# Storing the second product's weight forms three steps later

## The chip, the core and the metric

The kernel runs on one core of a Trainium2 chip. The metric is the device time of one execution in microseconds (us); the time of a kernel is the median of its runs. Profiles are taken from one execution; times in them count from the first instruction.

## What is computed

Attention with normalised queries and keys, and behind it a feed-forward layer with a squared ReLU. Inputs are float32, but the two weight matrices are float64.

```python
batch, n_heads, seq, head_dim = (8, 12, 448, 64)
q_n, k_n = (rmsnorm(q, g_q), rmsnorm(k, g_k))
scores = (1 / sqrt(head_dim)) * matmul(q_n, k_n.T)
attn = softmax(scores)                       # 1e-9 added to the sum
x = matmul(attn, v)                          # -> (8 * 448, 12 * 64) = (3584, 768)
h = maximum(x @ w_in, 0.0)                   # w_in  (768, 2048)
out = h * h @ w_out                          # w_out (2048, 768)
```

## The kernel before

**Attention and feed-forward interleaved.** Attention goes over 48 pairs of heads (8 batches of 6 pairs). The feed-forward layer works on two batches at a time (a group, `u` = 0 to 3), and for each group over 4 blocks of 512 hidden units. While TensorE works at the feed-forward layer of one group, the attention of later batches is woven between its matmuls. Only the first 13 pairs run with no feed-forward work beside them (`visit_alone`, up to about 140 us).

**Weight forms.** Both products of the feed-forward layer use a scheme in which four quadrants are multiplied with seven products in place of eight. It needs sums and differences of the weight quadrants, the "forms". A tile of forms of the second product, `out_sb[t]` with t = 0 to 7, is 128 x 8 x 384 float32: 4 quadrants and 4 derived forms, 1536 KB. Two tiles go with each block. `out_sb` has two buffers.

**How a tile is made, in the first group only.** Weights come as 64-bit words. `load_weights` (L1293) loads one quadrant into one of three buffers `words` (L1300 for w_in, L1305 for w_out); `split_words` takes the words apart on ScalarE (L1319 to L1321); `join_words` and `end_join` put a float32 together on VectorE (L1332, L1352, L1356). This is `convert`, once for each of 64 quadrants. After the fourth quadrant of a tile, `make_weight_forms` puts four sums into `sums_to_make` and, for a tile of the second product, one store into `forms_to_store`. `make_sum` then issues one sum a call (L1432, in turn on VectorE and GpSimd) and, when no sum is left, one store (L1434), from `out_sb[t]` to `out_forms[t]` in DRAM. The later groups read the forms back with `load_out` (L901, 24 loads), the first of them behind the last matmul of the first group. Forms of the first product are kept likewise in `in_deep`, with `deep_steps` (L1382 and L1384 the ready forms, L1392 a derived form on VectorE, L1410 its store).

**Steps.** Everything is issued in an order that the Python code fixes; each engine takes its own instructions in that order. All transfers but a few at the start are issued by SyncE's queue (SP), in order, and one that waits for a semaphore holds those behind it. There are two kinds of step:

- `begin(step)`, four times a pair while attention is alone: two calls of `make_sum`, then `follow_loads`, then `convert` where it is due.
- one round of `run(until)`, for every feed-forward product of 6 to 30 units of cost: a product's matmuls, a step of `deep_to_make`, `make_sum`, `follow_loads`, `end_join`, `convert` where due, loads of x rows (L805), attention tasks, and a few queued transfers of q, k and v (`follow_transfers`, shown as L325; while attention is alone they are issued at once, shown as L317).

**Counters.** `follow_loads` lowers the count of every entry of `to_load` and of `later` and issues those that have come to zero, first loads of words, then `later`, always from the head. `later` otherwise holds saves of x tiles (count 4, L731), stores of finished rows (count 2, L1264) and the `load_out` calls (count 4).

```python
        for some in later:
            some[0] -= 1
        while later and later[0][0] <= 0:
            later.popleft()[1]()
```

**What stands behind the weights.** ScalarE also computes the exponentials of attention (L453), VectorE also the accumulation of the second product (L1259), and TensorE waits for both to free its banks. Matmuls are L1024 and L970 (first product), L1202 and L1140 (second), L445 and L434 (scores), L535 and L549 (times v), L584 and L601 (sums of weights).

Of the kernel before, what the change touches and what calls it, by code (L numbers as in the profile page):

```python
# [224 lines left out]
def program(ctx, tc, rows, v, g, wide, ones, moe_w_in, moe_w_out, out, shift):  # L225

    nc = tc.nc
# [1056 lines left out]
    words, targets, sums_to_make, forms_to_store = {}, {}, deque(), deque()  # L1284
# [133 lines left out]
    def make_all_deep():  # L1418
        while any(callable(some) for some in sums_to_make):
            make_sum()  # L1420
        while deep_to_make:
            deep_to_make.popleft()()
# [3 lines left out]
    def make_sum():  # L1426

        if sums_to_make and callable(sums_to_make[0]):
            sums_to_make.popleft()()
        if sums_to_make:  # L1430
            to, left, right, op = sums_to_make.popleft()
            next(sum_engines).tensor_tensor(out=to, in0=left, in1=right, op=op)  # L1432
        elif forms_to_store:
            nc.sync.dma_start(*forms_to_store.popleft())  # L1434

    pieces, begun = iter(range(len(all_pieces) + 1)), []

# [13 lines left out]
    to_load, later = deque(), deque()  # L1451
# [52 lines left out]
    def run(until):  # L1504
        nonlocal spent, slowly
        slowly = True
        while spent < until:
            cost = next(stream)
            spent += cost
            if deep_to_make:  # L1510
                deep_to_make.popleft()()
            make_sum()
            follow_loads()
            end_join()
            while first and late and late[0] <= spent:
                late.popleft()
                convert()
            arrive()
            follow_plan(2 if first else 1)
            most = 2 if cost > COST_OUT else 1  # L1520
            run_tasks(most, 2 + len(transfers) // 8)
# [27 lines left out]
    def begin(step):  # L1549
        for _ in range(2):  # L1550
            make_sum()
        follow_loads()
        while early and early[0] <= step:
            early.popleft()
            convert()
            end_join()
# [247 lines left out]
```

## Time and profile before

| | us |
|---|---|
| median of 3 runs | 1425.24 |
| lowest and highest run | 1421.85, 1431.42 |
| profiled execution | 1425.5 |
| its span, first to last instruction | 1423.4 |
| mean granted TensorE clock | 0.993 |

The stretches of the profiled execution in which the stores lie, from the stage table (busy us of an engine in each stretch; the DMA share is the mean busy share of the 16 DMA engines):

| stretch, us | TensorE busy | VectorE busy | granted clock | DMA share |
|---|---|---|---|---|
| 80 to 100 | 20.00 of 20 | 18.02 | 1.00 | 0.47 |
| 100 to 120 | 16.47 of 20 | 14.97 | 0.83 | 0.68 |
| 120 to 140 | 19.44 of 20 | 15.50 | 1.00 | 0.60 |
| 260 to 280 | 19.63 of 20 | 17.53 | 1.00 | 0.93 |
| 280 to 300 | 15.37 of 20 | 15.73 | 1.00 | 0.71 |
| 360 to 380 | 17.33 of 20 | 17.60 | 0.91 | 0.92 |
| 380 to 400 | 18.89 of 20 | 12.93 | 1.00 | 0.61 |
| 460 to 480 | 18.43 of 20 | 18.88 | 1.00 | 0.94 |
| 480 to 500 | 18.11 of 20 | 12.25 | 0.83 | 0.85 |
| 500 to 1423 | 907.20 of 923 | 468.80 | 1.00 | 0.49 |

A row of a timeline reads: start, length, engine, line, operation, out<-in, shapes, how many, and in brackets the engine's idle time before it and what ended it. SPq is SyncE's queue; its length is the time of issuing, not that of the transfer.

### The profile page before, as it was taken

The numbers are of one execution on the slowest core, as the hardware profiler recorded it, in microseconds if no ns is written. First come the engines' busy times: TensorE is split into PE (matmuls) and PEld (weight loads), VectorE is DVE, ScalarE is ACT, GpSimd is POOL, SyncE is SP. The second block draws the span as 40 slices with busy tenths as digits, with TensorE's granted clock in tenths as the row PEclk, the third lists the DMA queues.
The fourth block names the chain that finished last, engine by engine and source line by source line (L and its number), as shares of the span: only waits on it lengthen the run. The fifth ranks groups of instructions, "written<-read, shape, count | busy, mean of one in ns | idle before, by whom it ended". The sixth has DMA issues, their size and how long they took to land.

```text
span 1423.4 us, 19419 instructions
## 1 busy us (share of the span) xinstructions
PE 1377.7 (97%) x6336; PEld 850.8 (60%) x6336; DVE 841.4 (59%) x1675; ACT 587.6 (41%) x1126; POOL 784.3 (55%) x778
## 2 busy tenths in 40 slices
PE   7998999989899999999999999999999999999998
PEld 3333444434344467585776758566675858778694
DVE  4997567877877775355455665445544565254444
ACT  6775456645546234433342434444243403221230
POOL 5666755564645696465485777655673554030311
PEclk9999999999999999999999999999999999999999
DMA  5555745966768957373654747465551716234132
GB/s 147 142 152 157 202 106 143 258 171 180 205 181 244 272 149 242 73 233 90 194 153 153 222 108 229 131 190 137 151 164 27 276 57 243 108 106 174 45 145 80
DMA packets 378931, 229.15 MB, mean 161 GB/s; under 512 B 271940, under 2 KB 347588, under 8 KB 374724
## 3 DMA queue, kind: packets, MB, share of 16 engines
q1 hardware_dynamic: 378528, 227.75, 55.2%
q8 instruction: 52, 0.85, 0.2%
q14 instruction: 59, 0.48, 0.1%
q10 hardware_dynamic: 292, 0.07, 0.0%
HBM read 172.49 MB, written 55.25 MB: 160 GB/s over the span
## 4 chain that ended last, share of the span: by engine, by line
PE 63%; POOL 3%; DVE 2%; DMA 2%; issue 2%; SPq 1%; ACT 1%; DVEq 0%; POOLq 0%; ACTq 0%
PE bank L1202 25%; PE bank L1024 20%; PE bank L1140 5%; PE bank L549 4%; PE bank L434 4%; PE bank L445 2%; PE bank L970 1%; POOL sum L472 1%; PE bank L535 1%; DMA in_sb<-in_deep 1%; PE bank L610 1%; PE bank L570 1%; DMA out_sb<-out_forms 0%; DVE acc L1259 0%; SPq L325 0%
## 5 line engine op out<-in xcount | busy, mean ns | idle before, releaser
L1024 PE MATMUL bank<-xT,in_sb 128*128 128x224 f32 x1344 | 289.5, 354 | 5.1 <-DMA in_sb<-in_deep 2.8
L1202 PE MATMUL bank<-out_sb,hid 128*128 128x384 f32 x768 | 271.0, 489 | 7.5 <-DVE acc L1259 5.8
L1259 DVE TENSOR_TENSOR acc<-acc,bank 128x384 f32<-128x384 f32 x324 | 173.0, 548 | 157.4 <-PE bank L1202 137.7
L1024 PEld LDWEIGHTS bank<-xT,in_sb 128*128 128x128 f32 x1344 | 252.4, 190 | 17.6 <-ACT wT L453 5.6
L453 ACT ACTIVATE wT<-bank,rr 128x448 f32<-128x448 f32 x288 | 164.1, 631 | 137.3 <-PE bank L434 74.3
L1202 PEld LDWEIGHTS bank<-out_sb,hid 128*128 128x128 f32 x768 | 144.5, 190 | 113.1 <-DVE acc L1259 9.8
L1202 PE MATMUL bank<-out_sb,sums 128*128 128x384 f32 x576 | 206.1, 490 | 1.7 <-DVE acc L1259 1.5
L203 POOL TENSOR_TENSOR rr<-ms,minus_half 128x8 f32<-128x8 f32 (+1 forms) x96 | 149.3, 1555 | 99.9 <-DVE ms L196 98.5
L1009 DVE TENSOR_TENSOR hid<-hid,bank 128x224 f32<-128x224 f32 x312 | 111.4, 384 | 87.8 <-PE bank L1024 83.5
L1202 PEld LDWEIGHTS bank<-out_sb,sums 128*128 128x128 f32 x576 | 107.7, 190 | 86.3 <-issue 4.2
L970 PE MATMUL bank<-xT,in_sb 128*128 128x448 f32 x336 | 131.9, 546 | 0.0
L472 POOL TENSOR_TENSOR sum<-sum,wT 128x448 f32<-128x448 f32 (+1 forms) x96 | 111.7, 1182 | 18.8 <-ACT wT L453 17.0
L1077 POOL TENSOR_TENSOR hid<-hid 128x448 f32<-128x448 f32 x24 | 27.4, 1141 | 160.2 <-DVE hid L1009 156.2
L445 PE MATMUL bank<-qT,kT 64*128 64x448 f32 (+1 forms) x492 | 107.1, 585 | 8.5 <-ACT qT L368 3.8
L472 POOL TENSOR_TENSOR sum<-wT 128x448 f32<-128x448 f32 x48 | 57.7, 1225 | 103.7 <-ACT wT L453 103.7
L970 PEld LDWEIGHTS bank<-xT,in_sb 128*128 128x128 f32 x336 | 62.1, 190 | 69.0 <-issue 62.5
L1140 PE MATMUL bank<-out_sb,hid 128*128 128x384 f32 x256 | 88.8, 493 | 0.0
L1081 ACT ACTIVATE hid<-hid 128x448 f32<-128x448 f32 x96 | 55.0, 573 | 75.3 <-DVE hid L1009 51.8
L193 DVE TENSOR_REDUCE ms<-squares 128x8 f32<-128x512 f32 (+1 forms) x68 | 41.8, 615 | 64.5 <-ACT squares L180 64.5
L445 PEld LDWEIGHTS bank<-qT,kT 64*128 64x128 f32 (+1 forms) x492 | 36.7, 170 | 71.1 <-issue 40.4
L1024 PE MATMUL bank<-more,in_sb 128*128 128x224 f32 x288 | 75.2, 355 | 3.2 <-DVE hid L1009 1.8
L434 PE MATMUL bank<-qT,kT 64*64 64x448 f32 x552 | 76.1, 541 | 0.8 <-ACT wT L453 0.8
(135 smaller groups left out, 2012.0 us busy)
## 6 DMA issues: line engine op xcount, KB each, us to landing
out_sb<-out_forms SPq DMA_DIRECT2D x24, 1536.0 KB, 9.7
in_sb<-in_deep SPq DMA_DIRECT2D x64, 384.0 KB, 3.8
in_sb<-in_deep SPq DMA_DIRECT2D x80, 256.0 KB, 4.1
words<-in_moe_w_in_dram SPq DMA_DIRECT2D x32, 384.0 KB, 3.7
words<-in_moe_w_out_dram SPq DMA_DIRECT2D x32, 384.0 KB, 3.5
out_forms<-out_sb SPq DMA_DIRECT2D x8, 1536.0 KB, 6.2
qk<-in_q_dram SPq DMA_DIRECT2D x96, 96.0 KB, 2.6
qk<-in_k_dram SPq DMA_DIRECT2D x96, 96.0 KB, 2.6
```

Source lines behind the costliest of these rows:

```text
L203: self.nc.gpsimd.tensor_tensor(out=self.rr[i][:, x, 0 : self.count(i)], in0=ms, in1=self.minus_half.to_broadcast(list(ms.shape)), op=ALU.pow,)
L434: nc.tensor.matmul(sc[ds(half * D, D)], lhsT=turned[i, 1][ds(e * D, D), ds(m * P + half * D, D)], rhs=turned[i, 0][ds(e * D, D), :], start ...
L445: nc.tensor.matmul(sc[some], lhsT=turned[p, 1][r, keys], rhs=turned[p, 0][r, :], start=True, stop=True,)
L453: nc.scalar.activation(new_weights((i, m), e), sc, AF.Exp, scale=rows.rr[i][:, 1, 2 * m + e : 2 * m + e + 1],)
L472: nc.gpsimd.tensor_tensor(out=sums[i, e][some], in0=left[some], in1=weights[key_of(i, m), e][some], op=ALU.add)
L549: nc.tensor.matmul(bank[ds(e * D, D), :], lhsT=values[i][keys, n, e, :], rhs=weights[(i, n), e][keys], start=n == 0, stop=n == NJ - 1 and ...
L970: nc.tensor.matmul(ps, lhsT=w_sb[:, IN.index(left), c, :], rhs=forms[u, c][right], start=first and c == 0, stop=c == NK - 1, skip_group_ch ...
L1009: nc.vector.tensor_tensor(out=quarter(name, n), in0=quarter(base, n), in1=ps, op=ALU.add)
L1024: nc.tensor.matmul(ps, lhsT=left, rhs=right, start=start, stop=stop, skip_group_check=True)
L1140: nc.tensor.matmul(ps, lhsT=hid[a].rearrange("p t e s -> p t (e s)")[:, t, ds(NT * P, P)], rhs=w_sb[t][:, 2 * a + half, :], start=(a, t) = ...
L1202: nc.tensor.matmul(ps, lhsT=lefts[left][:, t, ts(tt, P)], rhs=w_sb[t][:, OUT.index(right), :], start=first and t == 0, stop=t == 1, skip_g ...
L1259: nc.vector.tensor_tensor(out=acc, in0=acc, in1=ps, op=ALU.add)
```

## The change

One line of `make_sum` changes. The store of a tile is no longer issued there; it is put into `later` with a count of 3, and `follow_loads` issues it.

```diff
@@ -1431,7 +1431,7 @@
             to, left, right, op = sums_to_make.popleft()
             next(sum_engines).tensor_tensor(out=to, in0=left, in1=right, op=op)
         elif forms_to_store:
-            nc.sync.dma_start(*forms_to_store.popleft())
+            later.append([3, partial(nc.sync.dma_start, *forms_to_store.popleft())])
 
     pieces, begun = iter(range(len(all_pieces) + 1)), []
 
```

All eight stores take the new way, and nothing else is edited.

## The prediction

> **What bounds the kernel now.** I read the page first (busy times, slices, DMA issues), then the waits by engine, then the timeline around each of the eight stores, and last the stage table of the stretches in which TensorE stood still.
>
> ```profile
> PE 1377.7 (97%) x6336; PEld 850.8 (60%) x6336; DVE 841.4 (59%) x1675; ACT 587.6 (41%) x1126; POOL 784.3 (55%) x778
> ...
> PE   7998999989899999999999999999999999999998
> ...
> out_forms<-out_sb SPq DMA_DIRECT2D x8, 1536.0 KB, 6.2
> ...
> words<-in_moe_w_in_dram SPq DMA_DIRECT2D x32, 384.0 KB, 3.7
> ```
>
> TensorE is busy 1377.7 of 1423.4 us, so every stall of all kinds together is 45.7 us. The stores lie between 98.5 and 486.4 us; after that none is left, so the change can only act on what TensorE loses in about a third of the span. A store moves 1536 KB and lands in 6.2 us (248 KB per us); it is four times a load of weight words (384 KB, 3.7 us).
>
> I number the stores 0 to 7 by the tile they keep. They start at 98.54, 129.11, 270.07, 293.48, 365.37, 391.56, 459.06 and 486.35 us. Only two of them hold the queue by their own wait; the waits of SP between 90 and 100 us show the long one:
>
> ```profile
> SPq L1434 <- POOL out_sb L1432: 6.3, 1, 6.3
> ```
>
> The queue reached store 0 at 92.2 us and stood until the last sum on POOL was done at 98.5. What that costs is seen in the timeline behind it:
>
> ```profile
> 107.90 0.53 SPq L1305 DMA_DIRECT2D words<-in_moe_w_out_dram  x1
> ...
> 111.29 0.55 ACT L1319 ACTIVATE words<-words 128x384 f32<-128x384 f32 x1 [7.96 <-DMA words<-in_moe_w_out_dram]
> ...
> 112.74 1.14 ACT L453 ACTIVATE part<-bank,rr 128x448 f32<-128x448 f32 x2
> ...
> 113.41 4.08 PE L445 MATMUL bank<-qT,kT 64*128 64x448 f32 x12 [3.15 <-ACT part L453]
> ```
>
> The load of words was issued late, ScalarE stood 7.96 us for it, the exponentials queued behind it on ScalarE came late, and TensorE stood 3.15 us for them. The stage table for the same place shows a second cost (columns: stretch, length, busy PE, PEld, DVE, ACT, POOL, granted clock, DMA share, GB/s):
>
> ```profile
> 112.00:114.00 2.00, 0.59 (x2) 0.56 (x3) 0.00 (x0) 1.97 (x5) 0.00 (x0) 0.78 0.90 196
> 114.00:116.00 2.00, 2.00 (x8) 0.71 (x10) 0.08 (x1) 2.00 (x5) 0.00 (x0) 0.50 0.74 200
> ...
> 118.00:120.00 2.00, 2.00 (x12) 0.34 (x12) 1.97 (x4) 1.45 (x3) 1.82 (x3) 0.51 0.00 0
> ```
>
> After the stall the granted clock is 0.5 for six microseconds.
>
> **Where each store goes.** The count of 3 is lowered in the same call in which the store is queued, so the store leaves two calls of `follow_loads` later, behind that call's load of words. Counted along the code, and set beside SP's rows: store 0 passes eleven loads of v, q and k and the words load at 107.90. Store 1 passes nothing, since no transfer is issued in the two `begin` calls it waits: its place in the queue is the same. Stores 2, 4 and 6 are queued in the first products; each passes two in_deep stores of derived forms, four transfers of the attention inputs, and one words load (2 and 4) or two loads of x rows (6); each then stands just ahead of the last three in_deep stores. Stores 3, 5 and 7 pass three or four loads of q/k, and 3 and 5 also one words load and the save of an x tile, which was queued earlier and goes first. No entry of `later` holds a store back: the saves waiting there fall due in the step in which the store is queued. ScalarE, VectorE, POOL and TensorE keep their instructions and order. The forms are read back from 528 us on, and the two buffers of out_sb are written again some 40 us after a store, so no reader moves.
>
> **Store 0: a gain.** With the store gone from its place, SP can go on at 94.4, when the matmul on the old v tile (93.44 + 0.97) frees its buffer, instead of 98.96: the words load at 107.90 comes at about 107.90 - 4.5 = 103.4. Its buffer has been free since 97.6 (VectorE's last step on the words three pieces before). Landing 3.4 us later, as it did, gives 106.8, against 111.3. ScalarE's exponentials then end near 109.4 and TensorE, free at 110.26, does not wait: 3.15 us gone. The slow clock goes with it: twelve matmuls took 4.08 us against 2.70 for the same twelve at 90.81, the next four 1.76 against 0.92, and some 0.5 more in the following sums, 2.7 us in all. Against it: store 0 now stands ahead of the next words load (108.52 before, about 104 now), which lands behind it near 104 + 6.2 = 110.2; it is wanted near 115.75 - 5.9 = 109.9. I take off 0.9. **-5.0**, bounds -5.9 and -3.0 (if the clock still drops). *On the clock:* the Trainium skill (TensorE: Matmul & The Clock Gate, Part 1) says that the clock halves after an idle window of some 3.4 us and comes back after as long a busy one. By it the slow stretch would cost about 1.7 us, which would make this term -4.0. The rows show six microseconds at 0.5 behind a stall of 3.15 us, so I keep 2.7.
>
> **Store 2: a loss.** These are the rows behind it:
>
> ```profile
> 270.07 0.45 SPq L1434 DMA_DIRECT2D out_forms<-out_sb  x1
> ...
> 277.63 0.47 SPq L1410 DMA_DIRECT2D in_deep<-more  x1
> ...
> 281.20 0.51 SPq L1300 DMA_DIRECT2D words<-in_moe_w_in_dram  x1
> ...
> 285.22 0.56 ACT L1319 ACTIVATE words<-words 128x384 f32<-128x384 f32 x1 [3.60 <-DMA words<-in_moe_w_in_dram]
> ...
> 286.73 1.15 DVE L1332 TENSOR_SCALAR in_sb<-words 128x384 uint32<-128x384 uint32 x1
> ...
> 288.39 1.92 PE L1202 MATMUL bank<-out_sb,sums 128*128 128x384 f32 x4 [1.54 <-DVE acc L1259]
> ```
>
> The store moves to just behind 277.63. From 270 to 285 us the DMA engines are full, as their slices between 262 and 290 us (0.7 us each) show, and they were not quite full just before:
>
> ```profile
> DMA  7800939999579999999899999898989990000599
> ```
>
> What was issued from 270 to 277.6 without the store is 192 (v) + 192 + 384 (words) + 32 + 112 + 192 + 112 = 1.2 MB, 4.9 us of work in 7.5. So 2.6 us of full transfer is given up, and the words load of 281.20 lands at about 287.8 instead of 285.2. ScalarE's step on them ends at 288.4; VectorE, which took it at 286.73, comes 1.7 us late to the accumulation behind it, for which TensorE already waits (1.54). **+1.7**, bounds 0 (SP was slowed by the store, 1.3 us and more for single issues at 272.39 and 274.04, and may now be earlier) and +5 (the stall grows past the 2.45 us after which the clock fell to 0.5 at 376, costing some 2.7 more).
>
> **Store 4: nothing.** The same shift of 2.6 to 3 us meets the words load of 376.41, used at 380.45 by ScalarE, but by VectorE only at 386.26: about 5 us of cover, made by VectorE's own queue. Without that cover it costs 3. Bounds 0 and +3.
>
> **Store 6: a small loss.** It now stands ahead of three in_deep stores and nine loads of the first deep weights (2.5 MB, first used at 523). Behind them the load of k at 476.09 ended a wait of VectorE of 1.81 us at 481.88; 2.6 us more delays accumulations that TensorE needs next at 489.75, which ended at 484.3. **+1.0**, bounds 0 and +4.
>
> **Stores 1, 3, 5, 7: nothing.** Words at 298.20 and 397.19 go ahead of the store and land earlier; ScalarE stood 2.13 and 2.66 us for them, but TensorE is not behind that. Bounds -1 and 0 together.
>
> Sum: -5.0 + 1.7 + 0 + 1.0 = -2.3. The profiled execution took 1425.5 us, 2.1 more than its span, and would take 1423.2; the median of the runs is 1425.24, 0.3 under it, so **1422.9 us**. Own bounds: -5.9 - 1 = -6.9 and -3 + 5 + 3 + 4 = +9, so 1418 to 1434.
>
> **Rivals.** *No effect (about 1425):* the store still fills the engines for as long, and what is won at 110 us is lost to the words load behind the moved store. For it: every transfer stays. Against it: SP's 6.3 us wait surely goes.
>
> *Slower:* the moved stores 2, 4 and 6 stand straight ahead of loads that are wanted at once, and each passes its whole 6.2 us on, through ScalarE's or VectorE's in-order queue, to TensorE, with a clock drop of 2.7 each: 3 x 8.9 - 5 = +21.7, 1447 us. For it: three of the tightest stretches (15.4 of 20 us busy at 280 to 300) lie there, and ScalarE's waits for words total 48.0 us. Against it: the store only shifts by 8 us inside a run of transfers that is full anyway, and ScalarE has 4.87 us to spare at 296.74. It decides when words land more than 4 us later than now at two of the three places.
>
> *Faster by more:* all stalls near stores are due to their transfers and go: 5.9 at store 0, 4.5 between 284 and 293, 2.5 and 1.2 of clock at 375, 1.1 at 390, 3.2 and 2.9 of clock at 480 to 488: 21.3, 1404 us. Against it: the releasers named there are VectorE's accumulation, qT and a POOL sum, not a DMA.
>
> **How the numbers follow.** Forecast 0.52, no effect 0.23, slower 0.15, faster by more 0.10. About one per cent, 14 us, is what a measurement of this kernel can tell from no change. The first two lie within it, and a hundredth of each of the others: faster 0.09, within 0.77, slower 0.14. The range takes my own bounds, widened by the spread of the three runs (-3.4 and +6.2 about their median) and towards the two outer cases: 1413 to 1437.
>
> **What would show it.** Right: SP issues words near 103.4 instead of 107.90, the stall of 3.15 us at 113 and the 0.5 clock behind it are gone, store 0 no longer waits for POOL, store 1 still does; ScalarE's wait for words at 285 grows by about 2.6 us. Wrong: a new TensorE stall of over 4 us between 280 and 300 or 375 and 390 (the slower rival), or the stall at 113 still there with another releaser (no effect).

## The result, and the profile after

| | before | after |
|---|---|---|
| median, us (21 runs each) | 1425.24 | 1421.82 |
| lowest and highest run | 1421.85, 1431.42 | 1417.31, 1425.84 |
| profiled execution, us | 1425.5 | 1423.5 |
| its span | 1423.4 | 1421.7 |
| mean granted clock in it | 0.993 | 0.994 |

The ratio of after to before is 0.9973, with a 95% interval of [0.9962, 0.9984]: 3.4 us less at the medians, with an interval that lies below 1. The forecast was 1422.9.

The page of the changed kernel, its busy times, TensorE's slices and the stores' row:

```profile
PE 1377.9 (97%) x6336; PEld 851.7 (60%) x6336; DVE 839.5 (59%) x1675; ACT 587.3 (41%) x1126; POOL 783.7 (55%) x778
...
PE   7999999999899998999999999999999999999998
...
out_forms<-out_sb SPq DMA_DIRECT2D x8, 1536.0 KB, 6.3
```

The sums say almost nothing: busy times are the same, a store lands as slowly as before. In TensorE's row four slices differ from before: the fourth (107 to 142 us) was 8 and is 9, the ninth (284 to 320) too, and the fourteenth (462 to 498) and the sixteenth (533 to 569) were 9 and are 8. A slice says where to look, not what was won there: a TensorE with a slow clock is busy as well. So the ninth rises with a slow clock, and the fourteenth falls with less of it.

The changed kernel's timeline there, rows of SP, ScalarE and TensorE (start, length, engine, line; the idle time before, and its releaser, in brackets). L1462 is the line in `follow_loads` that issues what waits in `later`, and so the stores:

```profile
94.13 1.22 SPq L317 DMA_DIRECT2D vt<-in_v_dram  x2
...
101.26 0.53 SPq L1305 DMA_DIRECT2D words<-in_moe_w_out_dram  x1
101.89 0.38 SPq L1462 DMA_DIRECT2D out_forms<-out_sb  x1
103.41 0.38 SPq L1300 DMA_DIRECT2D words<-in_moe_w_in_dram  x1
...
105.04 0.59 ACT L1319 ACTIVATE words<-words 128x384 f32<-128x384 f32 x1 [2.07 <-DVE out_sb L1332]
...
112.02 0.97 PE L445 MATMUL bank<-qT,kT 64*64 64x448 f32 x4 [0.26 <-DVE qT L408]
```

SP goes on at 94.13 with no store in its way. The load of words that stood at 107.90 is issued at 101.26. ScalarE starts on those words at 105.04 where it was 111.29, and what it waited for is no longer the transfer, but VectorE. TensorE's stall of 3.15 us has become 0.26, with another releaser.

SP's waits in the same place, of the changed kernel, now hold one line for a store, and it is store 1 at 123.22:

```profile
SPq L1462 <- POOL out_sb L1432: 1.7, 1, 1.7
```

The stage table of the changed kernel (columns as in the prediction's):

```profile
112.00:114.00 2.00, 1.98 (x12) 0.57 (x16) 1.90 (x5) 1.68 (x4) 1.25 (x1) 1.00 0.52 176
114.00:116.00 2.00, 2.00 (x20) 0.62 (x14) 1.97 (x5) 0.15 (x1) 1.82 (x3) 1.00 0.22 51
...
284.00:288.00 4.00, 2.23 (x4) 0.91 (x4) 3.86 (x6) 1.56 (x3) 3.37 (x3) 0.52 0.34 53
```

The clock stays at 1.00 at 112 to 116 us, and TensorE does 20 matmuls in the stretch in which it did 8. But at 284 to 288 us the clock is 0.52, where the kernel before had 1.00 in all of 280 to 300.

To see where time comes and goes, I took the start of the same matmul in two profiles, the kernel's and that of before (TensorE's order is the same in all kernels of this study), and the difference of the two. The columns are times in the profile of before; the numbers are us that TensorE's work is ahead (negative) or behind:

```
at, us              108    122    160    180    283    295    470    600
after             -0.35  -5.68  -5.89  -5.58  -5.59  -3.62  -3.64  -1.97
store 0 alone     -0.34  -5.67  -5.88  -5.81  -5.82  -5.83  -5.85  -5.58
all but store 0   -0.63  -1.86  -2.29  -2.13  -2.15  -0.50  -0.51  -0.66
wait kept         -0.04  -3.47  -3.25  -3.35  -3.38  -1.92  -1.91  -1.78
store 0 by POOL   -0.16  -5.48  -5.70  -5.78  -5.79  -4.15  -4.14  -4.07
second copies     -0.16  -5.48  -5.69  -5.64  -5.64  -4.27  -4.28  -3.44
words first       -0.59  -6.00  -6.21  -6.25  -6.25  -6.25  -6.23  -8.49
stores 0 and 1    -0.36  -5.69  -5.90  -5.85  -5.87  -5.88  -5.87  -5.36
count 8           -0.18  -5.50  -5.71  +0.62  +0.61  +2.62  +2.59  +1.15
store 1 late      -0.19  -5.51  -5.72  -0.40  -0.42  +1.44  +1.40  +3.94
late but store 1  -1.25  -6.58  -6.79  -6.75  -6.76  -5.11  -5.12  -2.64
```

In the changed kernel 5.3 us are won between 108 and 122 us, and 2.0 are given back between 283 and 295. Nothing happens at store 4 or before store 6 (295 to 470). Another 1.7 go until 600 us, on balance: 1.3 are won behind 480, where the clock is slow for 3.4 us in place of 6.8 behind the same stalls, and 3.0 are lost near 555. The other rows are the experiments.

### The profile page after: what moved, and what is told of

Same layout as the page of the kernel before. It is cut to its first block, busy times and chain, and to the rows that moved or that the text cites. A ratio compares the mean times of both kernels' runs of the same rounds, so it can differ in the third digit from the quotient of the medians.

```text
span 1421.7 us, 19421 instructions
## 1 busy us (share of the span) xinstructions
PE 1377.9 (97%) x6336; PEld 851.7 (60%) x6336; DVE 839.5 (59%) x1675; ACT 587.3 (41%) x1126; POOL 783.7 (55%) x778
## 4 chain that ended last, share of the span: by engine, by line
PE 62%; POOL 4%; DVE 3%; issue 2%; DMA 2%; SPq 1%; ACT 1%; DVEq 0%; POOLq 0%; ACTq 0%
PE bank L1202 25%; PE bank L1024 20%; PE bank L1140 5%; PE bank L549 4%; PE bank L434 4%; POOL sum L472 2%; PE bank L445 1%; PE bank L970 1%; SPq L325 1%; DMA in_sb<-in_deep 1%; PE bank L610 1%; PE bank L535 1%; PE bank L570 1%; POOL xT L689 1%; DMA xT<-x_rows 0%
```

## The experiments

Kernels of one group ran on the same chip beside the kernel before: its median was 1425.44 us (32 runs) for the first four, 1424.55 (26) for the next four and 1424.33 (23) for the last two. In the edits, `t` is the number of the store.

**Store 0 alone.**

```diff
-            later.append([3, partial(nc.sync.dma_start, *forms_to_store.popleft())])
+            some, t = forms_to_store.popleft(), next(tiles_stored)
+            if t == 0:
+                later.append([3, partial(nc.sync.dma_start, *some)])
+            else:
+                nc.sync.dma_start(*some)
```

> Only store 0 goes through the count of 3; stores 1 to 7 stay where they were before. Theory (the gain is store 0's, the other seven cost a little): the whole gain of 4 to 5 us stays and the loss of 1 to 2 us behind stores 2 and 6 is not paid, so 4 to 6 us below the kernel before, ratio about 0.9965. Rival (the gain is spread over the eight stores): about an eighth to a half of 3.4 us, ratio 0.9985 or more. In the trace: no 3.15 us stall at 113 us, clock 1.00 between 112 and 120 us, and the same stalls as before from 260 us on, shifted.

Measured: 1420.61 us, ratio 0.9966 [0.9954, 0.9978]. Store 0 alone gives at least as much as all eight.

**All but store 0.** The same with `if t > 0`.

> Store 0 stays where it was; stores 1 to 7 go through the count of 3. Theory: the gain is gone and what stores 2, 4 and 6 cost is left: 0 to 3 us above the kernel before, ratio 1.000 to 1.002. Slower rival of the prediction (each of the three passes its whole transfer on): 14 us or more above, ratio 1.01. Gain spread over all: 2 to 3 us below, ratio 0.998. In the trace the 3.15 us stall at 113 us is there again with the clock at 0.5 behind it.

Measured: 1425.44 us, 0.9997 [0.9983, 1.0012]. The other seven give no gain, but they do not show the loss of 2.7 us either that the prediction's terms for stores 2 and 6 add up to: the interval reaches from -2.4 to +1.7. The stall at 113 us is back, and behind it the clock is slow for a shorter time than before:

```profile
112.88 3.93 PE L445 MATMUL bank<-qT,kT 64*128 64x448 f32 x12 [3.24 <-ACT part L453]
```

```profile
112.00:114.00 2.00, 1.12 (x3) 0.81 (x4) 0.00 (x0) 2.00 (x5) 0.00 (x0) 0.78 0.75 163
114.00:116.00 2.00, 2.00 (x10) 0.30 (x8) 0.62 (x1) 2.00 (x5) 0.00 (x0) 0.50 0.74 224
116.00:118.00 2.00, 2.00 (x16) 0.36 (x12) 1.90 (x6) 1.97 (x5) 1.65 (x1) 0.87 0.00 0
```

TensorE loses 1.2 us less there than in the kernel before (-0.63 to -1.86 in the table), with a stall that is no shorter.

**The change with the wait kept.** A store of 4 KB of the same tile stands at store 0's old place. It needs the same last sum of POOL, so SP stands as before, and the large store goes three steps later.

```diff
+            if t == 0:
+                nc.sync.dma_start(mark, some[1][:, 7, 0:8])
+            later.append([3, partial(nc.sync.dma_start, *some)])
```

> All eight stores go through the count of 3, but at the old place of store 0 SyncE issues a store of 4 KB out of the last sum of the same tile, so the queue still stands there for the sum on POOL, and the 1536 KB move later all the same. Theory (it is the wait in the queue that cost): the stall at 113 us comes back, SP issues the words load near 107.5 us again, time as e2, 0 to 3 us above the kernel before. Rival (the 1536 KB ahead of the words load cost): the stall is gone as in the change, 3 to 4 us below the kernel before; half and half: words load late by 4 us but landed sooner, stall about 1.5 us.

Measured: 1422.66 us, 0.9985 [0.9971, 0.9999]: neither all nor nothing. Its timeline (its lines from L256 on are one higher, from L1425 on two or more):

```profile
98.50 0.33 SPq L1438 DMA_DIRECT2D mark<-out_sb  x1
98.93 1.22 SPq L318 DMA_DIRECT2D vt<-in_v_dram  x2
...
106.06 0.53 SPq L1306 DMA_DIRECT2D words<-in_moe_w_out_dram  x1
...
109.76 0.56 ACT L1320 ACTIVATE words<-words 128x384 f32<-128x384 f32 x1 [6.46 <-DMA words<-in_moe_w_out_dram]
...
111.91 2.96 PE L446 MATMUL bank<-qT,kT 64*128 64x448 f32 x12 [1.69 <-ACT part L454]
```

SP stands until 98.50, as in the kernel before. But the eleven loads behind it take 7.1 us to issue (98.93 to 106.06), against 8.9 (98.96 to 107.90) behind the large store. So store 0 delayed the words in two ways: by 4.5 us for POOL's sum, and by 1.8 us because the loads behind it were issued more slowly. The second is what this kernel wins. Its stage table has one more surprise:

```profile
112.00:114.00 2.00, 2.00 (x10) 0.88 (x12) 0.19 (x1) 2.00 (x5) 0.00 (x0) 1.00 0.96 312
114.00:116.00 2.00, 2.00 (x15) 0.46 (x16) 1.51 (x4) 1.42 (x3) 0.61 (x1) 1.00 1.29 288
```

Behind a stall of 1.69 us the clock is not lowered at all. So 1.8 us of earlier issue are worth 3.4 in the table of offsets (108 to 122 us): 1.5 of stall, and the slow clock.

**Store 0 issued by GpSimd at its old place**, all else as before. The transfer is not delayed; only SP does not stand for it.

```diff
+            (nc.sync if t else nc.gpsimd).dma_start(*some)
```

> Store 0 is issued at its old place in the program, but by GpSimd, whose own sum it waits for, so SyncE does not stand and yet the 1536 KB start near 98.5 us; stores 1 to 7 as before. Theory (the wait in SyncE's queue cost): words load near 103 us, no or a small stall at 113 us, 3 to 5 us below the kernel before, less what issuing costs GpSimd. Rival (the 1536 KB ahead of the words load cost): the words load lands behind them, after 98.5 + 6.2 = 104.7 us plus its own transfer, and the stall shrinks by no more than half. A long issue on GpSimd (over 2 us) would show as later sums there and blurs the answer.

Measured: 1420.38 us, 0.9970 [0.9953, 0.9988]. The timeline of this kernel:

```profile
99.27 0.77 POOL L1436 DMA_DIRECT2D out_forms<-out_sb  x1
...
107.23 0.56 ACT L1319 ACTIVATE words<-words 128x384 f32<-128x384 f32 x1 [4.68 <-DMA words<-in_moe_w_out_dram]
```

The large transfer is issued at 99.27 us, ahead of the words (100.84) and not behind them. ScalarE still waits 4.68 us for the words. But it starts at 107.23, 4 us earlier than before, and that is early enough for TensorE. So the whole gain is there without moving the transfer, once SP need not stand for the sum. Moving it while SP stands, as in the kernel with the wait kept, gave 3.4 of the 5.3 us.

**A second copy of stores 2, 4 and 6**, behind the first, into a spare place: 3072 KB where the change has 1536.

```diff
             later.append([3, partial(nc.sync.dma_start, *some)])
+            if t in (2, 4, 6):
+                later.append([3, partial(nc.sync.dma_start, spare[t // 2 - 1], some[1])])
```

> The change, and behind each of the stores 2, 4 and 6 a second store of the same 1536 KB into a spare place, so that the transfers behind stand for one more 6.2 us; all else as the change. It measures how much lateness those places bear. Theory (a shift of about 1 us is covered by VectorE's own queue, a shift of 6 us is not): ScalarE's wait for words near 282 us grows from 5.4 to some 10 us, VectorE comes about 5 us late to the accumulations there, TensorE's 4.1 us of stalls grow to about 9; at store 4 a cover of some 5 us takes most of it; at store 6 up to 4 us: in all 5 to 12 us above the change, ratio to the kernel before 1.001 to 1.006. Rival (the stalls there are made by VectorE alone and bear anything): within 1.5 us of the change, ratio 0.997.

Measured: 1420.35 us, 0.9975 [0.9964, 0.9987]. My theory fell, and the rival held. ScalarE's and VectorE's rows behind store 2 in this kernel:

```profile
281.08 1.15 DVE L1332 TENSOR_SCALAR in_sb<-words 128x384 uint32<-128x384 uint32 x1
...
284.75 0.55 ACT L1319 ACTIVATE words<-words 128x384 f32<-128x384 f32 x1 [8.76 <-DMA words<-in_moe_w_in_dram]
...
287.70 0.34 DVE L1332 TENSOR_SCALAR in_sb<-words 128x384 uint32<-128x384 uint32 x1
```

ScalarE waits 8.76 us for the words, and VectorE does its step at 281.08 all the same, before ScalarE has begun on them. So that step belongs to the piece before, as the code has it too (`convert` joins the last piece before it splits the next), and the piece that is late is joined at 287.70. TensorE's stalls between 270 and 300 us stay at 4.5 us in this kernel, as in the kernel before.

**Only the words first.** All stores stay where they were. Only the load of words is issued ahead of store 0 (the loads of v, q and k still stand behind it).

```diff
             if t == 0:
+                behind_words.append(some)
...
+        if behind_words:
+            while to_load:
+                load_weights(to_load.popleft()[1])
+            nc.sync.dma_start(*behind_words.pop())
```

> All stores as in the kernel before, store 0 too, which waits in SyncE's queue for POOL; only one load of words, the one that came late at 107.9 us, is issued ahead of store 0. The v, q and k loads behind the store still come as late as before. Theory (the path of the stall is: queue stands, words late, ScalarE stands, exponentials late, TensorE stands): the whole gain, 4 to 5.5 us below the kernel before, ratio 0.9965, no stall at 113 us, the clock 1.00 behind it. Rival (the late q, k or v loads hold attention too): less than half of it, ratio 0.9985 or more, with a stall that ends on a transfer of q, k or v.

Measured: 1417.99 us (5 runs), 0.9959 [0.9943, 0.9974]. SP's waits between 88 and 100 us in this kernel:

```profile
SPq L1305 <- DVE out_sb L1356: 9.3, 2, 5.5
SPq L1565 <- POOL out_sb L1433: 0.4, 1, 0.4
```

SP stands until 97.95 us here too, but now 5.5 us of it for the buffer of the words and only 0.4 for the store's sum. The whole gain is there (-0.59 to -6.00 in the table), though the other loads behind the store are as late as before. It is the words, then ScalarE, then the exponentials, then TensorE, and nothing else that the queue held.

**Stores 0 and 1 delayed**, by counts of 3 and 5, so that store 1 no longer makes SP wait 1.7 us either; the others at their old places.

```diff
+            if t < 2:
+                later.append([3 + 2 * t, partial(nc.sync.dma_start, *some)])
```

> Store 0 with a count of 3, store 1 with a count of 5, which brings it past the v, q and k loads behind it and takes its own wait of 1.7 to 2.3 us out of SyncE's queue; stores 2 to 7 at their old places. Theory (a wait in the queue costs only where a load wanted soon stands behind it, and none does behind store 1): the same as with store 0 alone, ratio 0.9966. Rival (each wait of the queue costs its length): another 1.7 us off, ratio 0.9954.

Measured: 1419.62 us (9 runs), 0.9965 [0.9952, 0.9978]: like store 0 alone. The standing of a queue costs only what somebody behind it wants soon.

**A count of 8** for all stores in place of 3.

```diff
-            later.append([3, partial(nc.sync.dma_start, *forms_to_store.popleft())])
+            later.append([8, partial(nc.sync.dma_start, *forms_to_store.popleft())])
```

> All eight stores with a count of 8 in place of 3. Theory (what counts is that store 0 leaves its place; where the other seven go hardly matters): as the change, ratio 0.996 to 0.998. Rival (a store is best soon after it is ready, later places stand in the way of other loads): ratio 1.000 or more, with longer waits of ScalarE for words behind stores 3 and 5.

Measured: 1425.31 us, 1.0007 [0.9994, 1.0020]. The gain is gone, though not at store 0: the table has -5.7 at 160 us and +0.6 at 180. This kernel's rows of SP, VectorE and TensorE in between:

```profile
146.70 0.54 SPq L1462 DMA_DIRECT2D out_forms<-out_sb  x1
147.28 3.92 SPq L1382 DMA_DIRECT2D in_deep<-in_sb  x3
...
162.35 0.69 DVE L1392 TENSOR_TENSOR more<-in_sb 128x512 f32<-128x512 f32 x1 [10.14 <-DMA in_deep<-more]
...
165.72 4.85 PE L970 MATMUL bank<-xT,in_sb 128*128 128x448 f32 x6 [3.82 <-DVE hid L1110]
```

Store 1 now goes right ahead of the five stores of ready forms, behind which the first derived one is queued. VectorE stands 10.14 us until that one has left its buffer (6.66 us in the changed kernel), and TensorE stands 3.82 us for VectorE. It is much like the mechanism of the prediction's slower rival, at a store that I had counted at nothing for a count of 3.

**Store 1 late alone** (0 with a count of 3, 1 with 8, the others at their old places), and **all late but store 1** (a count of 8 for the seven others).

```diff
+            if t < 2:
+                later.append([3 + 5 * t, partial(nc.sync.dma_start, *some)])
```

```diff
+            if t != 1:
+                later.append([8, partial(nc.sync.dma_start, *some)])
```

> Store 0 with a count of 3, store 1 with a count of 8, the other six at their old places. Theory: the loss of the kernel with a count of 8 for all came from store 1 alone, issued at 146.7 us straight ahead of five in_deep stores, for which VectorE stood 10.14 us and TensorE 3.82. So this kernel gains some 5 us at 113 us, loses 6.3 us between 160 and 180 us, and ends near 1425.5 (ratio about 1.001), with VectorE's wait of some 10 us at 162. Rival: the loss was of the two together (the in_deep stores queue behind store 1 and behind what the other late stores push back), or of that one profile; then this kernel is like the one with stores 0 and 1 delayed by two and four steps, 1419.6 to 1421 (ratio 0.9966).

> All stores with a count of 8 but store 1, which is issued at its old place. Theory: store 1 was the only one that lost by standing eight steps late; the other six have cover wherever they stand. Gain at 113 us kept, no VectorE wait over 7 us at 162, no loss between 160 and 180 us: 1420 to 1422 (ratio 0.9966 to 0.998). Rival: stores 2 to 7 eight steps late lose too (the 2.0 us between 283 and 295 us, and more after 360): 1424 to 1426 (ratio 0.999 to 1.001).

Measured: 1427.18 us, 1.0016 [1.0002, 1.0030], for the first; 1421.00 us, 0.9973 [0.9959, 0.9987], for the second. VectorE's row in the first:

```profile
162.20 0.69 DVE L1392 TENSOR_TENSOR more<-in_sb 128x512 f32<-128x512 f32 x1 [10.00 <-DMA in_deep<-more]
```

The same step waits 6.39 us in the second. Between 160 and 180 us the first loses 5.3 us and the second nothing. So one store of the eight gained by going later, and one could have lost what the first won. For the other six no place tried here made a TensorE stall longer: between 268 and 500 us the stalls are the same in all twelve profiles to 0.1 us, but for one near 292 that is 2.2 us or up to 0.6 shorter.

## Why the prediction was right, and where it was not

**Store 0 (-5.0): right, in mechanism and nearly in size.** The trace has -5.3: 2.9 of stall (3.15 less 0.26) and 2.4 of clock, where I put 3.15 + 2.7 - 0.9. Three of its steps were off. That the size came out all the same is in part luck: the stall and the clock gave 0.5 less than I had, and the 0.9 was not paid. The words left at 101.26, not 103.4: I shifted the rows behind the store as they stood and missed that the store itself had slowed them (the wait-kept kernel: 7.1 us against 8.9). That was not needed: 107.23 on ScalarE was early enough in the kernel with store 0 on GpSimd's queue. The 0.9 for the next words load shrank: it was issued at 103.41, ScalarE waited 0.33 us for it, and TensorE for none of that. And one link changed hands, as ScalarE next waited for VectorE. The clock's part depends on the profile: with all but store 0 moved, a stall of 3.24 us was followed by 3.4 us of slow clock and cost 1.2 us less. The 2.7 from the rows came near the 2.4 of this pair of profiles, and with the other stretch the term would have been about -4.1 (5.3 less 1.2, an estimate). The estimate of 1.7 us by the rule of the Trainium skill (TensorE: Matmul & The Clock Gate, Part 1) lies between what the two stretches cost, 2.4 and about 1.2; they lasted 6.8 us and 3.4 us.

**Store 2 (+1.7): the step that failed is the pairing of two rows.** I wrote that VectorE "took it at 286.73", the words loaded at 281.20. The second-copies kernel shows that the step belongs to the words loaded one piece before. Those of 281.20 are joined at 293.36, as these rows of the kernel before show:

```profile
286.26 0.57 ACT L1321 ACTIVATE words<-words 128x384 uint32<-128x384 f32 x1
...
293.36 0.34 DVE L1332 TENSOR_SCALAR in_sb<-words 128x384 uint32<-128x384 uint32 x1
```

That is 6.5 us after ScalarE's last step on them ended, so a cover of 6.5 us stood where I saw a delay of 1.7. That ScalarE's wait grows was right: 3.60 to 5.42 us, 1.8 in place of 2.6. Nothing came of it. Even with a second copy it grew to 8.76, and VectorE's step at 287.70 still found the words done, 1.4 us before (285.77 + 0.56).

**What was lost at 283 to 295 us (2.0) is not this term**, though it looks like it. The stalls there are 4.1 us in the changed kernel and 4.5 before; what differs is the clock behind them. The kernel with store 2 at its old place and store 0 on GpSimd's queue loses 1.6 us there as well, with a clock of 0.89 and 0.69 in the two stretches of 4 us from 284. Store 0 alone, with the same stalls, has 1.00 and loses nothing. So the drop comes with these stalls in some profiles and not in others. All six kernels with store 2 moved show it (1.4 to 2.0 us lost), and two of the six with store 2 at its old place. Whether the moved store makes it likelier, or chance does, stays open: one profile of each kernel can't tell, and what decides it was not tried.

**Store 6 (+1.0): not there.** VectorE's wait there went from 1.81 to 2.06 us, and TensorE's three waits behind it are the same to 0.01 us (1.44, 1.77 and 0.23 now). **Store 4 (0): right in size, with the same wrong pairing.** The step at 386.26 belongs to the words loaded at 370.42; those of 376.41 are joined at 390.67, so the cover was 8.6 us and not 5. ScalarE's wait rose from 0.73 to 4.59 us, TensorE's next one stayed near 1.1. **Stores 1, 3, 5, 7: right.** Store 1 kept its place and its wait of 1.7 us, which costs nothing (the stores-0-and-1 kernel). But calling it harmless was true only for a count of 3.

**The sum.** With store 0's -5.3 and nothing for the rest it would have been 1425.5 - 5.3 = 1420.2, and store 0 alone took 1420.61. The median of the change, 1421.82, lies between that and the forecast. That the forecast came within 1.1 us of it is in part luck, since 2.7 us of it stand for two losses that did not come about as described. The interval of the change overlaps that of store 0 alone, so whether the seven other stores cost anything at a count of 3 stays open up to 1.7 us, the upper end for the kernel with all but store 0. Of the late losses in the profile of after, the largest is a TensorE wait for first-product weights read back from DRAM, at 553 us: 3.05 us against 1.71 before, with a slow clock behind it (0.66 from 556 to 560), 3.0 us in all. In the twelve profiles of this study it lies between 0.7 and 3.1, with no order by the stores' places (1.35 with stores 1 to 7 moved, 2.50 with 2 to 7 unmoved), so I do not put it down to the change.

**The rivals.** "No effect" fell at store 0: what was won there was not lost to the words load behind. "Slower" was right about its mechanism and wrong about its places; the price at store 1 was 6.3 and 5.3 us in the two kernels that paid it, clock included, not 8.9, and it needs a store straight ahead of transfers whose buffer VectorE wants next. "Faster by more" fell, since the stalls near 375 and 480 us (2.5 + 1.1 and 1.4 + 1.8) are there in both kernels, with their releasers.

## What to carry to other kernels

A transfer that must wait for its data is cheap itself and dear for what stands behind it in the same queue, so look for the first load behind it that an engine wants soon; here 4.5 us of standing were worth a stall and a slow clock, and moving that single load ahead (1417.99 us, five runs) did no less than moving all stores. A delayed transfer has to be followed to its new neighbours: three steps later none of the eight made a new stall of TensorE, eight steps later one stood ahead of stores on whose buffer VectorE waits. And before a late load is given a price, pair each load with the step that uses it by counting pieces, since rows that lie close in time can belong to different pieces.

## What the runs showed of the hardware

- **A large store slows the issue of what follows it.** The same eleven loads took 8.9 us to issue behind 1536 KB, 9.5 us in the words-first kernel (98.37 to 107.89), and 7.1 us without it (94.13 to 101.26 in the changed kernel, 98.93 to 106.06 with the wait kept). With the store on GpSimd's queue (99.27), SP's next load of words took 1.28 us to issue, against 0.53, so as far as one load shows the queue need not be the same.
- **A stall can cost twice, and its length alone does not say how much.** Behind 1.69 us TensorE's clock stayed at 1.00 (one profile). Behind the 2.45 us near 375 it fell to 0.5 in all twelve profiles. Behind some 4.5 us of stalls with short work between them, at 284 to 293, it fell in eight of the twelve. At 555, stalls of 2.42, 2.50 and 3.05 us lowered it, one of 2.56 did not. By the traces' records of the granted clock, each slow stretch between 80 us and the last 20 us of a span lasted 3.4 or 6.8 us, none anything else: 6.8 behind the stall of 3.15 us at 113 and 3.4 behind that of 3.24 (all but store 0), 6.8 behind 3.82 us at 165 (the count of 8) and 3.4 behind 3.68 (store 1 late).
- **Most of the scatter between runs goes with the clock.** Over the 21 runs of the changed kernel the time falls by 1.0 us for each 0.001 of mean granted clock (correlation -0.83). Time multiplied by one less the clock, an estimate of what slow clock takes, is 10.5 us in the mean of the 32 runs of before in the first group and 7.6 in that of store 0 alone: 2.9 of the 4.8 us between their medians.
